# Recurrent memory attention with a gated feed-forward product on one Trainium2 core: banks of the memory products, and the turn of k's map

## The chip, the cores and the metric

The kernel runs on one core of one Trainium2 chip. The core has five engines that each work through a queue of their own in order: TensorE (matmul; PE in the profile, its weight loads PEld), VectorE (DVE), ScalarE (ACT), GpSimd (POOL) and SyncE (SP, which here only issues transfers). Matmuls write into PSUM, eight banks of 128 x 512 fp32. The metric is the device time of one execution in microseconds; the kernel before has a median of 699.38 us over three runs (699.01 to 701.35).

## The reference

The input x is 2048 x 512. It is normalised, and two branches are computed from it: attention with a memory that is carried over four segments of 512 rows (32 heads of 16), and a feed-forward branch of 1792 columns with a ReLU. The output is x plus the product of the two.

```python
xn = _layernorm(x, axis=-1)
for s in range(N):                      # N = 4 segments of L = 512 rows
    logits = einsum("bhqd,bhkd->bhqk", qs, ks) * scale + mask
    a_dot = softmax(logits) @ vs
    pq = phi(qs)                        # phi(t) = t + 1 for t > 0, else exp(t)
    num = einsum("bhld,bhde->bhle", pq, M)
    den = einsum("bhld,bhd->bhl", pq, z)[..., None] + 1e-6
    o = g * num / den + (1.0 - g) * a_dot
    pk = phi(ks)
    M = M + einsum("bhld,bhle->bhde", pk, vs)
    z = z + pk.sum over rows
s = concat(o) @ wo
g = silu(relu(xn @ w1) @ w2)
return x + s * g
```

## The kernel before, in words

Everything is in fp32. Large matrix products are split into a high and a low part of each operand, so one product is three matmuls: high x high, high x low, low x high (`triple`, `lanes`). Each of these 128-row matmuls is again cut into a lower half (rows 0 to 63, L744) and an upper half (rows 64 to 127, L752), which run beside each other. The upper halves trail the lower ones through a queue of up to 14 (`back`); where the program must end a product at once it empties this queue, and the uppers then run without partners.

The work is cut into 16 blocks n = 4 s + g (segment s, group g of eight heads), each of two half blocks u = 2 n + q. For a block:

- `proj` multiplies x by 128 columns of wq and of wk. `projout` takes the result off its bank: ScalarE writes the high plane into a buffer F (L974), VectorE the low plane into another F (L975). Both are sent to DRAM (`sdq`, `sdk`; L978 the high plane twice, L979 the low one). There are four F buffers in all (`NF_ = 4`). phi of q (segments 1 to 3) and of k (segments 0 to 2) is made beside it (L984, L985, L992).
- `stack` fetches the planes back as score operands `qs`, `ks` (L1113). `rowmax` computes the scores once for the row maxima (L1139 on TensorE, two single banks at a time; L1145 on VectorE), which are transposed (L1163), sent out and back into `qs` (L1165, L1166).
- `expo` computes the scores again, transposed, into the **pair** `pt` of two banks (L1191), ScalarE takes the exponentials over both banks at once (L1202, L1208) and GpSimd cuts the triangle (L1198). `pv` multiplies by v (L1239) and ScalarE scales the result into a buffer F (L1254), from where it is sent to `nn` (L1262) and `dq` (L1267).
- For blocks of segments 0 to 2, `memory` turns phi(k) with VectorE (L1073) into `pkT`, and `memory2` multiplies it by v (32 matmul rows of L1096) and adds the result to the memory `MC` of its group.
- For blocks of segments 1 to 3, `spread` lays the memory and its denominators out in `MZ`, and `numden` multiplies phi(q) with it: numerators and denominators, one matmul each (L1025, L1026). ScalarE takes the numerators off (L1033, into the tile of phi(q)), VectorE the denominators (L1035, into a buffer F). From there they are sent on to the division in `combine`.

Of the eight PSUM banks, six are single (`ps`), two form the pair `pt`. Before the change `numden` writes the two halves of the pair.

The order of all this is written out: the kernel records operations and plays them back in an order that a table (`ORDER`) fixes; two more tables fix the bank of each result (`BANKS`) and the yes-or-no answers of the recording code (`CHOICES`), and `PLAN` the sequence of weight loads. Each engine's queue follows that order, so a wait at the head of a queue holds up what stands behind it. SP issues nearly all transfers, and a waiting transfer holds up the later ones. The costs in `KINDS` and the due times are only used where the tables are made, not in the run.

Of the kernel before, what the change touches and what calls it, by code (L numbers as in the profile page):

```python
# [8 lines left out]
F32 = mybir.dt.float32  # L9
# [7 lines left out]
L = 512  # L17
# [29 lines left out]
WARM = 1  # L47
ONPAIR = True
# [29 lines left out]
ORDER = (
    "0AzAyAxwFABtAsUEqVppVTnUTZkCSXhSWSeSgAiRRdAcdTbTfTWYACaOTYASTDALTQPLLEALL+AIOILEHKHIAGKBAJFbDADYDJHICJERNjGJAgDA"
    "eBdDCbbgbFaHDYPVGHYFMEVVNNCSMYUKORCTQBPQJOOaRUYSTWMQkMQnPkLNLiJagLXaQJXaAVNcXTTQWXJJPPTPIPJP3OASNLVHNOLJrHLeKAJ)"  # L80
    "AGGLIJJKJxKIIJLJOMIIGLJJGIPJKQKOLKLJGLIIHGIVGGLSGGPLGNGOMJJOKJKLJFVLIQNRF2FRJMIJFKJHsIVIHuI!toJnKJHImuLtHJdvIFdb"
    "GL%abfbv?oagsttapFng!rrnFg/k1YbJtxYjG3qY+ht+YrgFajhlWYygrgVqYecnYYkbalgdXdWamcbcaaiFZgciFdHTUaTXFpZeWmdbwkWZTRgT"
    "qlf2AViSQbyRSuZtcpVc^HRDlPW^CTDixRTviRSDtfQqQSDbvRnXUYSqjVfDQTRKPbQPZDwRbLe*!DYPpXD/Tn/vOntGNkGwMii7EhLEf2DKOJJG"
    "mdhE-FGa8GZVEgFs>GRdDkdmcHP5kqQkDY1z(YfkqYOXcZoGqlDZMmkbYlUOcgUNSbZYZFRQRWVDXdEOVQfQULJDvKT6JNOr2NUoDMHTkGzQitAQ"
    "JtqROFZSaFjZrwSWrtQoVoFVlNOFzVsRWOTCJSMnLn!LJJNkgN-eUdoQRCRP3PIX=jX0INexNJbJQZLJOoMNmNlCkPSPCeKDE6NubL5sQ2tLCxrt"
    "LVrsMoykUWvpMjhmLqhDjwCofthmtnfehfmiJdJsDkhePUmQSYQjc1WiEHSTvEcFRKX6QXpCW1PDm2akOT+LRRwxCRCt+SYqHA6BWFtOBTCNRNwD"
    "RJNtCVECIBFkBP&hRBL@EMiBJOCKIQCBSCQBQPCRJBTQIBNUSKNK2QCOINyJMqPRIOCfojecOqNapRimECqBfnimBxmwh0puyloh7nh+p58F5uMb"
    "B5uH/CBu3-91wFzWBX6vuF4j3sxxpwDtoTBrmapqTDnnBl2shtLmWMVmBirBWihIngvfklSr3jo1j2j7SizkJhRtiAAzzjwpWtjsJ7Vlqplb32Ov"
    "jyuxoeR8AFxbj6vw2jPVyAxgIDAEgXXeCEabKeZZBLZPYJLKYECAH#OGVCMLDFoAEpAqnMG3Czm1y{k0p)]mxkFB&u(Kt:E$!rE9[i]{/([pzp]$"
    "+7B)@,tDA5v2AB4/&978k?$66z>@By3c>Bb2pgA52k2BU0zVqUybkApuoall7xcyaTqmdUepildtTlkrbjyeYmnug5lfpBX3i06i0lYWvkXW1lwW"  # L90
    "dv^Ldo^JtjsV5SqAkh2jhkfrhqCejrZephccQuXjlQcpjkocAcPS6BaTSAa1OYsWANTBSMMSQnSQAKANMTALdMcLWO1OAWuKxt]vAR]1clA$y#p!"
    "IAz5n03BxmAjkALE+rk1ood5Aidkw0kdylKJuJ2lml1cnzmaxAQjYtiqrXmkjPIihabffDZ^ojh^mgroOeinFXgkB^aZifWWAW^QnXVAMXM^bSgV"
# [76 lines left out]
def emit(tc, PE, ACT, DVE, POOL, SP, cst, ps, dr, args):  # L169
# [30 lines left out]
    def dve(cols, rd, wr, fn, dl, per=1.05e-3):  # L200
        return S.op("DVE", 0.14 + cols * per, rd, wr, fn, dl)
# [1400 lines left out]
```

## Time and profile before

| what | value |
| --- | --- |
| median of the runs (lowest, highest) | 699.38 us (699.01, 701.35) |
| profiled execution: its own time, its span | 700.62 us, 698.9 us |
| TensorE, VectorE, ScalarE, GpSimd busy | 686.7, 497.6, 408.2, 448.5 us |
| mean granted TensorE clock | 0.996 |
| transfers | 141.46 MB in 126451 packets, mean 202 GB/s |

The span runs from the first to the last profiled instruction. A row of a timeline has its start in us, its length, engine, line, operation, output <- inputs and count, and in brackets the idle time ahead of it on its engine and what ended it. A row of the waits has the engine, its line and tile, what it waited for, and then total us, how often, and the longest. A row of the groups has a count, then busy time and mean ns of one, then the idle time before. A row of the chain of waits has its start, its length and what it is; a transfer there runs from its issue to its landing.

### The profile page before, as it was taken

How to read it: one execution, taken by the hardware profiler on the slowest of the kernel's cores; microseconds unless marked ns; L12 is line 12 of the kernel's file. 1: busy time of each engine (PE TensorE's matmuls, PEld its weight loads, DVE VectorE, ACT ScalarE, POOL GpSimd, SP SyncE). 2: the span in 40 equal slices, each digit the busy share in tenths (PEclk: the TensorE clock that was granted, in tenths of full speed). 3: DMA queues.
4: the chain of work that ended last, by engine and by line, in shares of the span. 5: the costliest groups of instructions: out<-in, count | busy, mean ns of one | idle time of the engine just before them, and what ended most of it. 6: DMA issues, size and time to landing. Idle time of an engine off the chain costs nothing.

```text
span 698.9 us, 18573 instructions
## 1 busy us (share of the span) xinstructions
PE 686.7 (98%) x6770; PEld 558.8 (80%) x6770; DVE 497.6 (71%) x1592; ACT 408.2 (58%) x621; POOL 448.5 (64%) x570
## 2 busy tenths in 40 slices
PE   9999999999999999999999999899999999999996
PEld 8898888777787797878788778698778978777775
DVE  4188988797879876587777878575857557656247
ACT  5545665655777664576566584655665555675721
POOL 4553674554656776684687957567575776666674
PEclk9999999999999999999999999999999999999999
DMA  5795567466668667765775577775567797754433
GB/s 167 224 298 177 190 202 231 138 183 216 204 224 250 205 201 248 250 211 177 226 244 151 178 236 237 256 207 173 164 188 217 222 306 233 231 179 135 113 82 121
DMA packets 126451, 141.46 MB, mean 202 GB/s; under 512 B 24904, under 2 KB 70216, under 8 KB 126360
## 3 DMA queue, kind: packets, MB, share of 16 engines
q1 hardware_dynamic: 126152, 140.07, 65.1%
q8 instruction: 54, 0.88, 0.5%
q14 instruction: 37, 0.30, 0.1%
q10 hardware_dynamic: 208, 0.20, 0.1%
HBM read 99.01 MB, written 34.93 MB: 192 GB/s over the span
## 4 chain that ended last, share of the span: by engine, by line
PE 79%; DMA 10%; DVE 3%; POOL 2%; issue 2%; ACT 2%; SPq 1%; DVEq 0%; POOLq 0%; ACTq 0%
PE ps L744 45%; PE ps L752 10%; PE ps L1239 8%; PE ps L1139 6%; PE pt L1191 5%; DMA sdq<-F 2%; DMA ks<-sdk 2%; PE pt L475 1%; DMA nn<-F 1%; DMA io<-in_B_w_dram 1%; DMA dd<-F 1%; PE pt L1025 1%; DMA out_dram<-io 1%; DVE none L1145 1%; DMA sdk<-F 1%
## 5 line engine op out<-in xcount | busy, mean ns | idle before, releaser
L1145 DVE CUSTOM_DVE_ANT_0 none<-ps,causal 128x512 bf16<-128x512 f32 (+3 forms) x512 | 249.5, 487 | 67.4 <-PE ps L1139 45.3
L411 POOL TENSOR_TENSOR wl<-io,wh 128x512 fp32r<-128x512 f32 x176 | 227.9, 1304 | 106.9 <-ACT wh L410 90.1
L1208 ACT ACTIVATE P<-pt 128x1024 f32<-128x1024 f32 x128 | 131.2, 1025 | 78.0 <-PE pt L1191 47.9
L752 PE MATMUL ps<-xl,wh 64*128 64x512 f32 x352 | 141.6, 402 | 0.0
L744 PE MATMUL ps<-xh,wh 64*128 64x512 f32 x352 | 141.3, 402 | 0.0
L752 PE MATMUL ps<-xh,wl 64*128 64x512 f32 x352 | 137.3, 390 | 0.0
L752 PE MATMUL ps<-xh,wh 64*128 64x512 f32 x352 | 136.9, 389 | 0.0
L744 PE MATMUL ps<-xh,wl 64*128 64x512 f32 x352 | 136.6, 388 | 0.0
L744 PE MATMUL ps<-xl,wh 64*128 64x512 f32 x352 | 136.5, 388 | 0.0
L410 ACT ACTIVATE wh<-io 128x512 fp32r<-128x512 f32 x176 | 106.1, 626 | 44.0 <-PE ps L752 27.1
L1198 POOL TENSOR_SCALAR_AFFINE_SELECT P<-P 128x512 f32<-128x512 f32 x128 | 80.9, 650 | 41.4 <-ACT P L1208 28.8
L744 PE MATMUL ps<-wh,hh 64*128 64x512 f32 x224 | 91.0, 406 | 0.0
L752 PE MATMUL ps<-wl,hh 64*128 64x512 f32 x224 | 90.4, 404 | 0.0
L744 PE MATMUL ps<-wl,hh 64*128 64x512 f32 x224 | 87.5, 390 | 0.0
L744 PE MATMUL ps<-wh,hl 64*128 64x512 f32 x224 | 87.2, 389 | 0.0
L752 PE MATMUL ps<-wh,hl 64*128 64x512 f32 x224 | 87.1, 389 | 0.0
L752 PE MATMUL ps<-wh,hh 64*128 64x512 f32 x224 | 87.0, 388 | 0.0
L1139 PE MATMUL ps<-ks,qs 64*128 64x512 f32 (+3 forms) x512 | 75.2, 336 | 1.6 <-DMA ks<-sdk 1.6
L1239 PE MATMUL ps<-P,vt 128*17 128x512 f32 (+3 forms) x1024 | 75.2, 434 | 0.0
L744 PEld LDWEIGHTS ps<-xh,wl 64*128 64x128 f32 x352 | 64.8, 184 | 7.4 <-issue 0.2
L1191 PE MATMUL pt<-qs,ks 64*128 64x384 f32 (+3 forms) x512 | 67.9, 310 | 2.9 <-DVE F L1035 2.7
L744 PEld LDWEIGHTS ps<-xh,wh 64*128 64x128 f32 x352 | 64.9, 184 | 6.9 <-issue 2.2
(179 smaller groups left out, 1764.4 us busy)
## 6 DMA issues: line engine op xcount, KB each, us to landing
io<-in_B_w_dram SPq DMA_DIRECT2D x112, 256.0 KB
qs<-sdq SPq DMA_DIRECT2D x32, 512.0 KB
ks<-sdk SPq DMA_DIRECT2D x32, 512.0 KB
sdq<-F SPq DMA_DIRECT2D x16, 512.0 KB
sdk<-F SPq DMA_DIRECT2D x16, 512.0 KB
io<-in_A_x_dram SPq DMA_DIRECT2D x28, 256.0 KB
io<-in_A_wv_dram SPq DMA_DIRECT2D x16, 256.0 KB
io<-in_A_wq_dram SPq DMA_DIRECT2D x16, 256.0 KB
```

The source lines that it names most:

```text
L410: act(512, [rk], [hk], lambda: ACT.activation(h, raw, AF.Copy), 7.0 + nsplit if early else 6.0)
L411: pool(512, [rk, hk], [lk], lambda: POOL.tensor_tensor(l, raw, r32(h), op=OP.subtract), 8.5 + 1.3 * nsplit if early else 25.4)
L475: PE.matmul(pw[:, :128], ident, ident, start=True, stop=True)
L744: i = PE.matmul(m[0], m[2][0][LO], m[2][1][LO], start=m[4], stop=False)
L752: PE.matmul(h[0], h[2][0][HI], h[2][1][HI], start=False, stop=h[5] is not None)
L1025: PE.matmul(pn, MZ[:64], f[:64], start=True, stop=True)
L1139: PE.matmul(two[a][0][:, o:o + w], qs[r, p, w - 128:w], ks[r, p, :w], start=True, stop=True)
L1145: dve(w + 40 + TTR, [pk, "causal"], [f"{dk}.{p}{a}{j}"], lambda p=p, j=j, o=o, w=w, a=a, pS=pS: DVE.tensor_tensor_reduce(none[:, :w], pS[: ...
L1191: PE.matmul(pT[:, a, o:o + w], ks[r, p, 128 * i:128 * i + 128], qs[r, p, 128 * i:], start=True, stop=True)
L1198: pool(512, ks, ks, lambda: POOL.affine_select(t, t, pattern=[[0, 4], [1, 128]], compare_op=OP.is_ge, fill=0.0, base=0, channel_multiplier ...
L1208: act(1024, tk, [both[p]], lambda: ACT.activation(P[:, 2 * p:2 * p + 2, :], pT, AF.Exp, scale=0.25), 18.5)
L1239: PE.matmul(pO[32 * b:32 * b + 17, 128 * i:], v, P[:, b, o:o + w], start=i == 0, stop=i == 3)
```

## The change

Three things change. First, `numden` takes two of the six single banks (`PDR.take(2)`) where it took the two halves of the pair, and the recording code asks for two more ready banks there (`ONPAIR = False`). Second, `memory` turns k's map by another way: one VectorE transpose of all 32 x 32 blocks in place of sixteen of 32 x 128, which leaves the blocks in the wrong partitions; the map then goes to DRAM in one transfer (`KDR`, two buffers) and comes back in four, each of which brings the blocks of 32 partitions to their place. `memory2` reads it under other indices; its matmuls are the same in size and number. Third, the four tables are new, and with them the order of the whole program.

```diff
-ONPAIR = True
+ONPAIR = False
...
+    KDR = Ring("kd", [128, L], F32, 2, dr)
...
-        (pn, nk), (pd, dk) = PDR.fixed(6), PDR.fixed(7)
+        (pn, nk), (pd, dk) = PDR.take(2)
...
-        tks = [f"{tk}.{a}{b}" for a in range(4) for b in range(4)]
-        pv = pk.rearrange("p (t a j) -> p a t j", a=4, j=32)
-        for i, k in enumerate(tks):
-            a, b = slice(32 * (i // 4), 32 * (i // 4) + 32), slice(32 * (i % 4), 32 * (i % 4) + 32)
-            dve(140, fk, [k], lambda a=a, b=b, i=i: DVE.transpose(pkT[a, :, b], pv[b, i // 4]), 4.0)
+        tks = [f"{tk}.{a}" for a in range(4)]
+        d, k = KDR.next()
+        dve(512, fk, tks, lambda: DVE.transpose(
+            pkT.rearrange("p a (t i) -> p a t i", i=32), pk.rearrange("p (t a j) -> p a t j", a=4, j=32)), 2.0)
+        dma(tks, [k], lambda: SP.dma_start(d, pkT.rearrange("p a n -> p (a n)")), 4.0, "put")
+        for a in range(4):
+            dma([k], [tks[a]], lambda a=a: SP.dma_start(
+                pkT[32 * a:32 * a + 32], d[:, 128 * a:128 * a + 128].rearrange("(b j) n -> j b n", b=4)), 4.0, "tr")
...
-                    PE.matmul(pm[r, :32], pkT[:, c, r], V[:, c, hd:hd + 2, 0:16],
+                    PE.matmul(pm[r, :32], pkT[:, b, 32 * c:32 * c + 32], V[:, c, hd:hd + 2, 0:16],
...
-    "fffbc60001aab2ab2abaaeaaba1041ebedd93ac75ddbdbecbf67c5ddc082777673bb1cef73bfef79f95fbcf8fbdeeabbe1dd8eee87f0fbbb"
+    "fffbc60001aab2ab2abaaeaaba1041ebedd93ac75dd9f77b3f6f3d7bbb9777767389dcef7773773fe7c9f7bdd77bdeef39c4ee76f7bc790f"
```

Line numbers shift: below the tables a line of the changed kernel up to `numden` is one lower (L974 is L973), from `memory2` on two higher (L1191 is L1193, L1254 is L1256). How the rows move is shown at three places.

ScalarE around the seventh taking-off of numerators (block 10, segment 2); `wh` are weights' high parts, `P` exponentials, `F` the buffers for planes and results. Before:

```order
L1208 ACTIVATE P_0_171<-pt 128x1024
L410 ACTIVATE wh_102<-io_124 128x512
L1208 ACTIVATE P_0_172<-pt 128x1024
L410 ACTIVATE wh_101<-io_123 128x512
L410 ACTIVATE wh_104<-io_125 128x512
L1254 ACTIVATE F_174<-ps_117,gsc 128x512
L1033 ACTIVATE pq_150<-pt,tiny,gcol 128x512
L410 ACTIVATE wh_103<-io_126 128x512
```

With the change:

```order
L1256 ACTIVATE F_176<-ps_116,gsc 128x512
L984 ACTIVATE pk_152<-pk_152 128x512
L409 ACTIVATE wh_101<-io_122 128x512
L1210 ACTIVATE P_0_173<-pt 128x1024
L409 ACTIVATE wh_104<-io_126 128x512
L1210 ACTIVATE P_0_174<-pt 128x1024
L409 ACTIVATE wh_102<-io_125 128x512
L1032 ACTIVATE pq_150<-ps_119,tiny,gcol 128x512
```

The scaled result of `pv` (L1254, now L1256) stood right ahead of the numerators and now stands seven rows ahead of them.

TensorE at the same place. Before:

```order
L1025 MATMUL pt<-pq_150,mz 128x512
L1026 MATMUL pt<-pq_150,mz 128x512
L744 MATMUL ps_115<-xh_128,wh_100 128x512
L752 MATMUL ps_116<-xl_130,wh_106 128x512
L744 MATMUL ps_115<-xl_130,wh_100 128x512
L752 MATMUL ps_116<-xh_128,wl_113 128x512
L744 MATMUL ps_115<-xh_128,wl_107 128x512
L752 MATMUL ps_116<-xh_128,wh_106 128x512
L1139 MATMUL ps_119<-ks_84,qs_81 128x256
L1139 MATMUL ps_118<-ks_84,qs_81 128x256
```

With the change:

```order
L1024 MATMUL ps_119<-pq_150,mz 128x512
L1025 MATMUL ps_118<-pq_150,mz 128x512
L743 MATMUL ps_116<-xh_128,wh_103 128x512
L751 MATMUL ps_115<-xl_130,wh_105 128x512
L743 MATMUL ps_116<-xl_130,wh_103 128x512
L751 MATMUL ps_115<-xh_128,wl_112 128x512
L743 MATMUL ps_116<-xh_128,wl_110 128x512
L751 MATMUL ps_115<-xh_128,wh_105 128x512
L1193 MATMUL pt<-qs_82,ks_85 128x384 x2
L1193 MATMUL pt<-qs_82,ks_85 128x128 x2
```

Before, twelve more half matmuls follow and then L1191, the next to write the pair. With the change the pair is written right there, and the next to write one of the two single banks is L743 on `ps_119`, after six more halves and four matmuls of L1141.

The first map on VectorE. Before:

```order
L992 SCALAR_TENSOR_TENSOR pk_152,zs_153<-ps_116,pk_152 128x512
L785 SCALAR_TENSOR_TENSOR hl_138<-ps_119,hh_132 128x512
L1073 STREAM_TRANSPOSE pkT_160<-pk_152 32x4x32 x10
L785 SCALAR_TENSOR_TENSOR hl_139<-ps_115,hh_133 128x512
L1073 STREAM_TRANSPOSE pkT_160<-pk_152 32x4x32
L785 SCALAR_TENSOR_TENSOR hl_140<-ps_118,hh_134 128x512
```

With the change:

```order
L991 SCALAR_TENSOR_TENSOR pk_152,zs_155<-ps_114,pk_152 128x512
L1070 STREAM_TRANSPOSE pkT_162<-pk_152 128x512
L784 SCALAR_TENSOR_TENSOR hl_138<-ps_119,hh_132 128x512
L784 SCALAR_TENSOR_TENSOR hl_141<-ps_115,hh_135 128x512
L784 SCALAR_TENSOR_TENSOR hl_139<-ps_117,hh_133 128x512
```

Sixteen rows became one. On SP's queue the changed program has five rows more for each map; around block 6's planes they stand so (`kd` is the map in DRAM, `io` a load of weights or gate):

```order
L1264 DMA nn_180<-F_177 16x512 x3
L1074 DMA pkT_162<-kd_154 32x4x128
L1264 DMA nn_180<-F_177 16x512
L978 DMA sdq_144<-F_179 128x512
L977 DMA sdk_146<-F_176 128x2x512
L1074 DMA pkT_162<-kd_154 32x4x128 x2
L978 DMA sdk_146<-F_177 128x512
L1115 DMA qs_81<-sdq_144 128x2x512
```

One part of the map stands between results of `pv`, two between the planes of k.

More of the change, by code (lines that the diff above doesn't have):

```diff
@@ new lines @@
+    "b9c8eebb87abeeceee2773bbcfbe7def97df3bbaee1beec77779dc1f7cfdef8efb9dfeceebfbde7b3bbbb1ceef3ef9f7bef7bc11dd57c776"
+    "77713b9ff73fe7defbde7ef29f7bdd777777ce09cee9dcbbbbe73fe5f75de52beeceeeec77773e7ee77dcefefffe6c07bb2bb11998860576"
+    "4bb29d9d97609b0036598d88d93fd86cf5db393b2a765d903b2ec93184d86c26d8cb30821b0f5ca552ed9711b188d80e72ed93332360d714"
+    "a5d886c236079be360d86d98d83609b0b63611b041b08d8f576c9ce5c5764b950413662cc6cf5764bb29db39762bb2982c188c218f5712e2"
+    "9c570abffe0")
@@ new lines @@
+BANKS = (
+    "0123456454034120513413124015210523051453067350672506712675426751436750673136750067256751212367426742367026745067"
+    "4211672467345674025672540256720132670236702067245674546714367315671506751672156713453670406724367452673436715216"
+    "7151670056754231672436710413041356735267026745267306755306700367132672131671346730504236732506732567015672416753"
+    "4304213675067425671305567436725042367136705067316751367125467255672426704046704367405516740067412673506710672450"
+    "6741567010674134671236754254012054301556754467426734067256723513672346703367545067216750510126712546725567216742"
+    "1673404254122675367355673054670316743203670367433670467504671551672067121670303673026703401167355673021674167552"
+    "6712246743167346703306743067235167012673104567243675136714004105267031673526723346730674541670306712567536723367"
+    "1442672126712167050567303670525670546705132674336720674025670146745167350167026735026753267467673670567267467167"
+    "6753301472316")
@@ L78 @@
 ORDER = (
[L79 to L88, printed above, removed]
@@ new lines @@
+    "SNOUSQRcQEeaPReaaRXZbUSXWVTRfASMdPPPSMLYVOVNwTTDuSSMUVPKOlfSgihhgDVecfQckdDLebcOchbaRfheIddYfXkbDMcaaaMebbMHLWbV"
+    "YLYUZbZYIZWVjVAVHYSTGHQZENEEWPejMVcKLKIYPJIDMaLQC?PCWOUVQcCSPPYCOXQVPOOHQQGCFIKEKNKJCQDNGIWGCHGVEGJFCgEVHQIUEETS"
+    "GJPTWOGURESHCUCMCEQNKLULLEKEcCdHaLkMCaYPKYCVHULCcGDQecQTCcPZYZHCgjEpghWMnVCQjCkhPWfgMVDUDRacjOCPPWeSYPMHTRPWKYI_"
+    "FNNJUCMXPSPLGPHNiP0UJfTSJcHJIZZCHXXHOLCEVCKRSKKPDDJObDMNYCCLKCFRKGFPLTEMNQIMNMFLMKIGSMJQJGGOHMJarHRADHFEEFMQEJEJ"
+    "cIBXwdBuCbFgCBX1XUCyRZdUUEend4CBbGjOEmgvYNmXjtBM0MUsqEYWcCrYVXXSmfWebKkbafjfRZeReccYbDwXsDYsUJWTNbmdKWBiLfBfFTwW"
@@ new lines @@
+    "hmbsgBRcGnbQQGKYHhdTeNGLVbHXUPWaWUYURSoVYOQkgZHYWGduUeUUUnNGcfViGKcfjdfgcAShfcdjhcSVYVdcAIaXI^SJXR^RIVZXV^MQWOIU"
+    "N^GTIReTSMZALPO{W^dLN^dN(AR%OMMKLKJAIBYHCYWGAHWUBERUARDUDDBNNW%o%TCRM?MhCdKPrftqNSqvNMomao3CnY0WczJOxrJ4ubpd3Aca"
+    "ylwoa?kmoaMb-jMwflBgZAjUHYTGkWNtGUaHwpPSGsmAQkPpPPOmJNejMMRvUFqauWUqYSoFVmjkFQUXNNSPAKgYZNKEVaIUcGWMVYGVXDGCWSJT"
+    "RSAPCTSOAAGRrRGEJCSEDBQPIFBFGKFPFAMFETEEENDGkLeiKPDgOcqHZJMFlaWL-LUaDJXJ@qDVAnUCVUaXPSZGWqbEVpNaETUXBaSTMRWBKDaV"
+    "SDLbSCRKXMQNUPVAFQbU:LJVMWJESPSEKLJOJJIURK^QQRWMJPJI@NKIPL^COGMMCJKDOJIEBDJAEhHC=GBCEjbBHmACAkdsCjBpA0gEAAwQcruv"
@@ L118 @@
+    "CULABFFIFHAGeJAdcFEcCZUAaXDaYIABXKSVAXAWZAYDRDjOUPgQNOiOhPJUAWNABTAJPFIAEAJEEAIACAEEBGDBDDFBAAAEEBACEABBBACABAAA")
 RSTEP = (((0, 3, 0),), ((0, 0, 0), (0, 2, 128)), ((0, 1, 0), (1, 1, 256)), ((1, 0, 0), (1, 2, 128)), ((1, 3, 0),))
```

69 lines of the change are left out of this document (26 added, 43 removed), and 2 rows, old and new, of the table KINDS.

## The prediction

> **What bounds the kernel now.** I read the page's busy times and its chain first, to see whether one engine sets the end; then the waits of TensorE alone, to see how little of its time is idle and who causes that; then the timeline around the longest of those waits.
>
> ```profile
> span 698.9 us, 18573 instructions
> PE 686.7 (98%) x6770; PEld 558.8 (80%) x6770; DVE 497.6 (71%) x1592; ACT 408.2 (58%) x621; POOL 448.5 (64%) x570
> PE 79%; DMA 10%; DVE 3%; POOL 2%; issue 2%; ACT 2%; SPq 1%; DVEq 0%; POOLq 0%; ACTq 0%
> ...
> PE pt L1191 <- DVE F L1035: 2.7, 2, 2.1
> PE ps L1139 <- DMA ks<-sdk: 1.6, 2, 0.8
> ```
>
> TensorE is busy for 686.7 of 698.9 us and carries 79% of the chain that ended last. Its list of waits is short: the largest entry (total us, times, longest) is the score matmul of L1191, which writes the pair of banks, held up by the VectorE eviction of the denominators at L1035, twice. The change removes no matmul, so what it can win is TensorE's waits and any slot that holds half a matmul pair; what it does to VectorE's 497.6 us counts only where TensorE waits for it.
>
> The longest wait, by the timeline:
>
> ```profile
> 444.66 0.39 PE L744 MATMUL ps<-xh,wh 64*128 64x512 f32 x1
> 444.89 0.39 PE L744 MATMUL ps<-xl,wh 64*128 64x512 f32 x1
> 445.11 0.39 PE L744 MATMUL ps<-xh,wl 64*128 64x512 f32 x1
> 445.35 0.69 ACT L1254 ACTIVATE F<-ps,gsc 128x512 f32<-128x512 f32 x1 [2.08 <-DMA sdq<-F]
> 445.93 0.77 ACT L1033 ACTIVATE pq<-pt,tiny,gcol 128x512 f32<-128x512 f32 x1
> 446.74 0.81 DVE L1035 TENSOR_SCALAR F<-pt,gcol,tiny 128x512 f32<-128x512 f32 x1 [3.20 <-ACT pq L1033]
> 447.60 0.79 PE L1191 MATMUL pt<-qs,ks 64*128 64x384 f32 x4 [2.10 <-DVE F L1035]
> 448.84 0.63 PE L744 MATMUL ps<-wh,hh 64*128 64x512 f32 x1
> 449.27 0.63 PE L744 MATMUL ps<-wl,hh 64*128 64x512 f32 x1
> 449.69 0.62 PE L744 MATMUL ps<-wh,hl 64*128 64x512 f32 x1
> ```
>
> Read upwards from 447.60: the score matmuls wait for both banks of the pair; L1035 empties one and is the second of two evictions that take turns; L1033 empties the other but stands in ScalarE's queue behind L1254, and L1254 stood 2.08 us because its buffer F was still being sent out. That transfer is the first row here; the others are used below.
>
> ```profile
> 438.97 6.29 DMA sdq<-F
> ...
> 161.45 4.72 DMA sdk<-F
> 166.23 4.75 DMA ks<-sdk
> ...
> 185.27 2.13 DMA sdq<-F
> ```
>
> It landed at 445.26. Then the second cost of the wait: before it a matmul pair starts every 0.23 us, after it every 0.43. The stretches (length, TensorE, weight loads, VectorE, ScalarE, GpSimd, granted clock, DMA share, GB/s) show why:
>
> ```profile
> 420.00:440.00 20.00, 20.00 (x196) 16.49 (x192) 17.90 (x59) 9.48 (x16) 11.79 (x16) 1.00 0.81 246
> 440.00:460.00 20.00, 17.90 (x190) 13.81 (x188) 10.63 (x39) 11.96 (x18) 15.23 (x16) 0.91 0.67 216
> ```
>
> The granted clock fell to 0.91 on average, so 0.09 x 20 = 1.8 us of clock were lost. The other wait on L1035 is shorter and costs no clock:
>
> ```profile
> 276.60 0.69 ACT L1254 ACTIVATE F<-ps,gsc 128x512 f32<-128x512 f32 x1 [1.83 <-DMA sdq<-F]
> 277.86 0.39 PE L744 MATMUL ps<-wh,hl 64*128 64x512 f32 x1
> 278.85 0.50 PE L1191 MATMUL pt<-qs,ks 64*128 64x384 f32 x4 [0.59 <-DVE F L1035]
> ```
>
> **The change part by part.** *Pair to two single banks.* The first wait cost 447.60 - 445.11 - 0.23 = 2.26 us and 1.8 us of clock, about 4.0; the second 278.85 - 277.86 - 0.23 = 0.76. Together 4.8 us, the most this part can give. It gives nothing if the wait goes to whoever needs the single banks next: in the new order that is a score-maximum matmul (L1141) or a chain, after about as little TensorE work as before (at the place shown in the order, twelve half matmuls and two groups of score matmuls now, eighteen halves and one group then). And a new wait of this sort elsewhere would cost 4.0 again, so the bounds are a gain of 4.8 and a loss of 4.0. What decides is ScalarE's queue, since the cause was a buffer F in flight. In the old order L1254 stands right ahead of the eviction; in the new one its counterpart L1256 stands seven rows ahead. Counting TensorE's rows at the trace's paces, I estimate that the F buffer of this L1254 was refilled 5 us of TensorE work after it was filled; in the new order no L1256 follows a plane's transfer by under 10 us. The long case should not come back. The short one had an estimated 15 us, and two L1256 near these matmuls now have 14, so I leave its 0.76 us in. I take a gain of 4.0.
>
> The Trainium skill ("TensorE: Matmul & The Clock Gate", section Why this matters for your kernels) says that gaps of TensorE up to about 3 us leave the clock alone. By it the 2.10 us wait would have cost 2.26 us and no clock, and the gain would be 2.3 instead of 4.0. The trace disagrees: the clock fell after a wait of 2.10 us, so the row is used.
>
> *Half pairs.* The old order runs the queue of upper halves (L752) dry once in mid-program: six uppers without partner, then six lowers. The new order does this only at the start and the end, as the old one also does.
>
> ```profile
> 555.72 0.39 PE L752 MATMUL ps<-wh,xh 64*128 64x512 f32 x1
> 555.94 0.39 PE L752 MATMUL ps<-wl,xh 64*128 64x512 f32 x1
> 556.62 0.39 PE L752 MATMUL ps<-wl,xh 64*128 64x512 f32 x1
> 556.75 0.40 PE L744 MATMUL ps<-wh,oh 64*128 64x512 f32 x1
> ```
>
> From 555.94 the uppers are alone until the first lower starts at 556.75: 0.81 us. Six slots of 0.23 = 1.4 us would be the upper bound, nothing the lower. I take 0.8.
>
> *One transpose for sixteen.*
>
> ```profile
> L1073 DVE STREAM_TRANSPOSE pkT<-pk 32x128 f32<-32x128 f32 x192 | 58.1, 303 | 4.5
> ...
> L1163 DVE STREAM_TRANSPOSE mT<-mm 128x32 f32<-128x32 f32 x32 | 6.6, 207 | 10.8 <-POOL mm L1154 10.6
> ```
>
> Row length sets the time: 128 columns take 303 ns and 32 take 207, so 1.0 ns a column; 512 columns come to 303 + 384 = 687 ns. Twelve make 8.2 us where 192 x 303 ns = 58.1 stood: VectorE loses 49.9 us, which lie beside TensorE's work. Of TensorE's waits above only L1035's name VectorE, and those come from ScalarE. I take nothing; bounds 0 and a gain of 1.4 us (half the 2.7).
>
> *Sixty more transfers on SP's queue.* Twelve maps go out whole (256 KB) and come back in four parts of 64 KB. The legs are dependent. The nearest rows are the planes' transfers above, twice as large, at 2.13 to 6.29 us a leg; two legs, the transpose and five issues make some 6 to 16 us. From k's last projection matmul to the map's first use the new order has at least 28 us of TensorE work (an estimate from its rows at the trace's paces; 25 in the old order), so the work of chains and scores covers the route; if that cover goes, the whole rest shows, at the memory matmul. What stands behind the transfers in SP's queue matters more.
>
> ```profile
> SPq L399 <- POOL wl L411: 50.9, 36, 6.7
> ...
> SPq L979 <- DVE F L975: 9.3, 8, 2.3
> ...
> 451.66 0.37 SPq L1113 DMA_DIRECT2D ks<-sdk  x1
> 444.17 0.59 SPq L1166 DMA_DIRECT2D qs<-mx  x1
> ```
>
> An issue takes 0.37 to 0.59 us, so sixty are 22 to 35 us, and SP has that room: it stands 50.9 us on one reason alone. A transfer to DRAM waits for its VectorE result at the head of the queue for 1.2 us on average (9.3 over 8). Late are then weight loads, score planes and maxima. Only three of the sixty stand between a k plane's transfer and its stack load, where the two legs of 4.72 and 4.75 us leave little: 3 x 0.59 = 1.8 us at worst (thirteen stand behind q's planes, which are ready earlier). Traffic rises by 12 x 0.5 MB = 6 MB. I take nothing; bounds 0 and a loss of 1.8.
>
> *The rest of the new order.* The stack loads' wait (1.6 us) is taken as unchanged.
>
> Sum: 4.0 + 0.8 = 4.8 us less. Of the span that is 698.9 - 4.8 = 694.1; the profiled execution took 700.62 in all, so 695.8. The median of the runs before is 699.38, 1.24 under the profiled one, and I forecast for the median: **694.6 us**.
>
> **The rivals.** *More comes off.* Both evictions' waits (4.8), the half pairs at their bound (1.4) and the waits on stack loads (1.6) go: 7.8 us, 691.6. For it: VectorE's 49.9 us also shorten what ScalarE and SP wait for. Against it: L1139's waits end at a transfer, and transfers increase. Chance 0.17.
>
> *The wait only moves.* The next user of a single bank waits as the scores did, or ScalarE stands at L1256 and holds the exponentials: the 4.0 comes back, the half pairs' 0.8 stays: 698.6. For it: the same two evictions still follow the same matmuls as closely. Against it: the greater distance of F's refills. Chance 0.20.
>
> *VectorE stands at F; slower.* F has four buffers. The new order has VectorE write k's lower plane (L974) into the buffer of q's upper plane, in two places, an estimated 3.3 us of TensorE work after q's was done; the closest such case in the old order has 5.9. q's plane must first be sent out, 2.13 to 6.29 us after an issue. With the median of those rows (4.7) and an eviction and an issue of 0.5 us each VectorE would stand some 2 us, with the maxima of L1147 behind it, whose banks TensorE needs. It decides where VectorE stands longer than the 2 us or so of work before such a bank's next use; then a wait costs what the one at 447.60 did, 4.0. Two of these, one at a denominator that reuses F after 1.3 us, and 1.8 on SP make 13.8: 694.6 + 13.8 = 708.4; with two of the three, 704.4. Against it: the old order has a denominator's F reused after 0.9 us, without a wait on TensorE. Chance 0.19.
>
> **How the numbers follow.** Forecast 0.44, more 0.17, moved 0.20, slower 0.19. Of the forecast's cases 0.02 end within 0.3% of before, which is about what a measurement of this kernel can tell from no change (2.1 us: 697.3 to 701.5). So faster 0.42 + 0.17 = 0.59, the same 0.22, slower 0.19. The forecast's own range is 692 to 697: the half pairs' bounds, and the short wait gone or doubled. The range for 8 in 10 reaches down past the first rival by its unknown VectorE gain and up into the slower case as far as one 4.0 wait over before: 689 to 703.
>
> **What would show it.** Right: no TensorE wait on L1034 or L1032 over 1 us, granted clock 1.00 between 420 and 480 us, twelve transposes of about 0.69 us, no wait of the memory matmul (L1098) on a transfer. Wrong: a TensorE wait of about 2 us on any engine with a clock under 1.00 beside it, or VectorE idle before L974 with a plane's transfer as the cause. The forecast is wrong if TensorE's busy time does not fall under 685 us (686.7 less the 1.8 of clock).

## The result, and the profile after

The changed kernel took 695.37 us (median of 6 runs, 692.75 to 699.18) beside 699.64 us for the kernel before on the same chip: a ratio of 0.9950, 95% interval 0.9927 to 0.9972. Two later timings of the same two kernels gave 0.9956 (0.9938 to 0.9974) and 0.9941 (0.9920 to 0.9963). So it is faster by 0.4 to 0.6%, 3.1 to 4.1 us in the three timings; the forecast was 694.6. One of the eight executions of the second timing took 834.03 us at a mean granted clock of 0.754 and is left out of its ratio.

The profiled execution of the changed kernel is the slowest of its six (699.18, span 697.5). First two lines of its page, then the waits of TensorE (total us, times, longest; three dots stand for rows left out):

```profile
span 697.5 us, 18533 instructions
PE 684.1 (98%) x6770; PEld 563.7 (81%) x6770; DVE 449.2 (64%) x1412; ACT 407.8 (58%) x621; POOL 448.5 (64%) x570
```

```profile
PE ps L1141 <- DMA ks<-sdk: 1.9, 3, 0.7
PE ps L1141 <- issue: 1.8, 3, 0.8
PE ps L1141 <- DMA qs<-sdq: 1.6, 1, 1.6
...
PE ps L743 <- DVE md L1147: 1.1, 1, 1.1
PE ps L1141 <- DMA io<-in_B_w_dram: 0.7, 1, 0.7
PE ps L1098 <- DMA pkT<-kd: 0.3, 1, 0.3
```

The wait of the exponentials' scores on the denominators' eviction, 2.7 us before, is not in this list, and nothing has taken its place at the evictions of the single banks (L1032, L1034). VectorE is 48.4 us less busy. What has grown is L1141, the matmuls that need the stack loads: 6.0 us where the profile of before had 1.6 (3.5 of the 6.0 name a stack load, 1.8 name nothing that the profile shows). The memory matmul L1098 waited once for a returned map, 0.3 us. The clock around the place of the old wait, and the transposes (length, TensorE, weight loads, VectorE, ScalarE, GpSimd, granted clock, DMA share, GB/s; then busy us and mean ns of one):

```profile
440.00:460.00 20.00, 20.00 (x233) 16.35 (x226) 13.90 (x46) 12.77 (x19) 14.27 (x16) 1.00 0.84 256
```

```profile
L1070 DVE STREAM_TRANSPOSE pkT<-pk 128x512 f32<-128x512 f32 x12 | 8.5, 706 | 0.0
```

The missing wait of the pair, the clock and the transposes are as forecast. The growth at L1141 and the wait of L1098, short as it is, are not. Whether the missing wait is the reason for the gain is another matter: one profile of each kernel can't say whether the old wait was there in other executions too.

### The profile page after: what moved, and what is told of

Read it like the earlier page. It is cut to its first block, busy times and chain, and to the rows that moved or that the text cites. A ratio compares the mean times of both kernels' runs of the same rounds, so it can differ in the third digit from the quotient of the medians.

```text
span 697.5 us, 18533 instructions
## 1 busy us (share of the span) xinstructions
PE 684.1 (98%) x6770; PEld 563.7 (81%) x6770; DVE 449.2 (64%) x1412; ACT 407.8 (58%) x621; POOL 448.5 (64%) x570
## 4 chain that ended last, share of the span: by engine, by line
PE 82%; DMA 9%; DVE 3%; SPq 2%; issue 2%; POOL 1%; ACT 1%; DVEq 0%; POOLq 0%; ACTq 0%
PE ps L743 41%; PE ps L751 16%; PE ps L1241 8%; PE ps L1141 5%; PE pt L1193 4%; DMA ks<-sdk 3%; DVE none L1147 2%; PE ps L1024 1%; PE pt L474 1%; DMA dd<-rq 1%; PE ps L699 1%; SPq L1264 1%; DMA kd<-pkT 1%; PE ps L700 1%; DMA io<-in_B_w_dram 1%
## 5 line engine op out<-in xcount | busy, mean ns | idle before, releaser
L1147 DVE CUSTOM_DVE_ANT_0 none<-ps,causal 128x128 bf16<-128x128 f32 (+3 forms) x512 | 249.8, 488 | 85.2 <-PE ps L1141 60.5
L743 PE MATMUL ps<-xh,wh 64*128 64x512 f32 x352 | 141.7, 403 | 1.1 <-DVE md L1147 1.1
L743 PE MATMUL ps<-xl,wh 64*128 64x512 f32 x352 | 136.7, 388 | 0.0
L743 PE MATMUL ps<-xh,wl 64*128 64x512 f32 x352 | 136.5, 388 | 0.0
L743 PE MATMUL ps<-wh,hh 64*128 64x512 f32 x224 | 89.9, 401 | 0.0
L743 PE MATMUL ps<-wl,hh 64*128 64x512 f32 x224 | 86.9, 388 | 0.0
L743 PE MATMUL ps<-wh,hl 64*128 64x512 f32 x224 | 86.9, 388 | 0.0
L1141 PE MATMUL ps<-ks,qs 64*128 64x384 f32 (+3 forms) x512 | 73.3, 331 | 6.0 <-DMA ks<-sdk 1.9
L784 DVE SCALAR_TENSOR_TENSOR hl<-ps,hh 128x512 fp32r<-128x512 f32 x56 | 38.2, 686 | 54.8 <-ACT hh L783 54.4
L743 PEld LDWEIGHTS ps<-xh,wh 64*128 64x128 f32 x352 | 65.0, 185 | 8.8 <-issue 2.6
L743 PEld LDWEIGHTS ps<-xh,wl 64*128 64x128 f32 x352 | 64.8, 184 | 7.2
```

Source lines behind the costliest of these rows:

```text
L743: i = PE.matmul(m[0], m[2][0][LO], m[2][1][LO], start=m[4], stop=False)
L784: dve(512, [pk, hk], [lk], lambda: DVE.scalar_tensor_tensor(hl, ph, 0.0, r32(hh), op0=OP.max, op1=OP.subtract), 10.6)
L1141: PE.matmul(two[a][0][:, o:o + w], qs[r, p, w - 128:w], ks[r, p, :w], start=True, stop=True)
L1147: dve(w + 40 + TTR, [pk, "causal"], [f"{dk}.{p}{a}{j}"], lambda p=p, j=j, o=o, w=w, a=a, pS=pS: DVE.tensor_tensor_reduce(none[:, :w], pS[: ...
```

## The experiments

Most of the edits change the order in which the same operations are issued: the list of operations that the table of numbers has put in order goes through a small function before it is issued. Their kernels have a few more lines, so line numbers are shifted; the operation's tiles tell which is which. Operations that such a function has to find carry a tag (`S.tag`), and not all lines that set a tag are shown. Of timelines only the rows that bear on the reading are shown. Gains in us are 699 times (1 - ratio), with the ratio's interval.

**Was the wait a property of the kernel? The transfer moved.** In the kernel before, one transfer alone is issued elsewhere: the send of q's upper plane of block 11, for whose buffer F the ScalarE instruction L1254 had stood 2.08 us.

```diff
+def rearranged(seq):
+    late = next(x for x in seq if x[1] == ("hi", 11, "q"))
+    out = []
+    for x in seq:
+        if x is not late:
+            out.append(x)
+        if x[1] == ("plane", 11, "q"):
+            out.append(late)
+    return out
```

> The kernel before, with one transfer moved and nothing else: the send of q's upper plane of block 11 (L978, sdq<-F), which the profile of before has issued at 438.97 us and landed at 445.26, and on which ScalarE's L1254 stood for 2.08 us, is issued right behind the ScalarE instruction that writes that plane. Theory A (the recorded one: the buffer F in flight caused the wait of the pair and the loss of clock): no wait of L1191 on L1035 of about 2 us near 447, granted clock 1.00 in 440 to 460, some 3.5 to 4 us less, 695.5 to 696 where before has 699.4. Rival B (VectorE's 58.1 us of transposes are what delays the eviction L1035): the wait stays, 699.4. Rival C (the time goes to the next wait in the chain, so a single wait is worth nothing): the wait is gone and the time within 1 us of before.

Measured: ratio 0.9997 (0.9976 to 1.0017), a gain of 0.2 us, between -1.2 and 1.7. By the time this is rival C. The place itself did change. ScalarE's counterpart of L1254 is L1273 here, the evictions are L1052 and L1054:

```profile
444.79 0.68 ACT L1273 ACTIVATE F<-ps,gsc 128x512 f32<-128x512 f32 x1
445.37 0.78 ACT L1052 ACTIVATE pq<-pt,tiny,gcol 128x512 f32<-128x512 f32 x1
446.18 0.81 DVE L1054 TENSOR_SCALAR F<-pt,gcol,tiny 128x512 f32<-128x512 f32 x1 [0.54 <-ACT pq L1052]
```

```profile
440.00:460.00 20.00, 20.00 (x233) 15.34 (x226) 14.19 (x50) 14.53 (x21) 16.76 (x17) 1.00 0.81 262
```

L1273 stands no more, L1052 follows at once, the clock is whole. Set beside the profile of before, matmul by matmul, this execution was 2.0 us behind at 418 us and 1.8 us ahead at 451: 3.8 us came off in this place, as forecast. But it had lost 2.0 us ahead of it, in other waits, and its span is 698.2 against 698.9. So either the time goes elsewhere whenever a wait is taken away, or the profile of before had an execution with an uncommonly long wait; the comparison of two single executions can't tell.

**Two more profiles of the kernel before** decide between these.

> The kernel before, unchanged, for a second profiled execution. Theory A (the wait of the pair near 447 us, 2.26 us and 1.8 us of clock, is the kernel's own): L1191 waits there for L1035 again by 1.5 us or more, with pairs of matmuls every 0.43 us behind it. Theory D (formed after the moved transfer gave no time: the wait depends on how long one transfer takes in one execution, and other executions lose as much elsewhere): in at least one of this profile and the next the wait is under 1 us and the clock whole, with a span still within 1% of 698.9.

> The kernel before, unchanged, for a third profiled execution. Theories and numbers as for the second: A has the wait near 447 us at 1.5 us or more in each profile, D has it under 1 us in at least one of them, at a span of 692 to 706.

The same place in the second and the third profile (spans 695.1 and 697.4 us):

```profile
442.25 0.69 ACT L1254 ACTIVATE F<-ps,gsc 128x512 f32<-128x512 f32 x1 [0.24 <-DVE md L1145]
442.84 0.77 ACT L1033 ACTIVATE pq<-pt,tiny,gcol 128x512 f32<-128x512 f32 x1
443.65 0.81 DVE L1035 TENSOR_SCALAR F<-pt,gcol,tiny 128x512 f32<-128x512 f32 x1 [0.87 <-ACT pq L1033]
444.57 0.45 PE L1191 MATMUL pt<-qs,ks 64*128 64x384 f32 x4
```

```profile
443.54 0.69 ACT L1254 ACTIVATE F<-ps,gsc 128x512 f32<-128x512 f32 x1 [1.03 <-DMA sdq<-F]
444.12 0.77 ACT L1033 ACTIVATE pq<-pt,tiny,gcol 128x512 f32<-128x512 f32 x1
444.93 0.81 DVE L1035 TENSOR_SCALAR F<-pt,gcol,tiny 128x512 f32<-128x512 f32 x1 [1.67 <-ACT pq L1033]
445.79 0.50 PE L1191 MATMUL pt<-qs,ks 64*128 64x384 f32 x4 [0.55 <-DVE F L1035]
```

The order of the chain is the same each time: L1254, L1033, L1035, L1191. Its length is not: ScalarE stood 2.08, 0 and 1.03 us for the transfer (in the second profile L1254 did not wait for it), TensorE 2.10, under 0.25 and 0.55 us. This is theory D. Only the first was long enough to cost clock. Over the kernel, TensorE's waits on L1035 were 2.7, 0.3 and 1.5 us in the three profiles. The place is the kernel's own, the size is that of one execution, and the mean over three profiles, clock included, is (2.7 + 1.8 + 0.3 + 1.5) / 3 = 2.1 us, half of what the forecast took.

The record has more than three executions for the clock, since each timed one is listed with its mean granted clock. A loss of 1.8 us in a span of 699 us leaves at most 0.9974. In the timings beside the experiments the kernel before has 0.999 or 1.000 in 34 of 51 executions, so at least two in three had no such loss; the changed kernel has this in all 20 executions that its three ratios use. On average 0.8 us of clock were lost before (0.9 with the transfer moved) and 0.2 with the change, the end of the program included, so the clock makes some 0.6 us of the gain.

**VectorE's time in the old order.** The kernel before with a single transpose, fifteen left out and no transfers.

```diff
-        for i, k in enumerate(tks):
...
-            dve(140, fk, [k], lambda a=a, b=b, i=i: DVE.transpose(pkT[a, :, b], pv[b, i // 4]), 4.0)
+        turn = lambda: DVE.transpose(
+            pkT.rearrange("p a (t i) -> p a t i", i=32), pk.rearrange("p (t a j) -> p a t j", a=4, j=32))
+        for i, key in enumerate(tks):
+            S.tag = ("none" if i else "turn", n)
+            dve(140, fk, [key], turn, 4.0)
```

> The kernel before, its order and its pair kept, with a single transpose of 512 columns where the first of the sixteen stood and the other fifteen left out, and no transfer added (so the 32x32 squares are not put in their places, and the sum over earlier blocks is another). It gives VectorE the 49.9 us without the transfers, in the old order; the new order without the transfers took 693.9. Theory A (VectorE's time is off the path): 698.5 to 700. Rival B (VectorE's time is the gain): 693 to 695.5. Between them, 695.5 to 698.5, both have a share: the order and the single banks have what lies between this time and 693.9.

Measured: 696.76 us, ratio 0.9966 (0.9951 to 0.9980): a gain of 2.4 us, between 1.4 and 3.4. It lies between the two theories, so both have a share. VectorE's 50 us were not free: about 5% of them shows. Its one profile has 0.6 us of waits on L1035's counterpart, against 2.7, 0.3 and 1.5. All idle time of TensorE between its first and last matmul is not less (5.0 us against 5.8, 3.8 and 4.5), but its busy time is: 684.7 us where the profiles of before have 686.7, 685.0 and 686.6. As a matmul of 0.39 us starts every 0.23 us, a delay of up to 0.16 us stays hidden in the busy time, so many delays too short for the list of waits may have gone; that they did is not shown one by one.

**VectorE's time in the new order.** The changed kernel with sixteen transposes again, one behind each VectorE instruction that follows the first, and without the transfers.

```diff
+        sixteen = [lambda a=a, b=b: DVE.transpose(
+            pkT[32 * a:32 * a + 32, :, 32 * b:32 * b + 32], pv[32 * b:32 * b + 32, a])
+            for a in range(4) for b in range(4)]
...
+        if tag and tag[0] == "turn":
+            owed = [("DVE", None, f) for f in EXTRA[tag[1]]]
+        elif eng == "DVE" and owed:
+            out.append(owed.pop(0))
```

> The changed kernel with its order and its single banks, but the map made the old way: sixteen transposes of 32x128, the first where the one stood and one more behind each following VectorE instruction; the five transfers per map are left out. Theory A (the gain is the order's and the banks', the map is neutral): the changed kernel's time, 695.4 with 1.5 us to either side. Rival B (VectorE's 49.9 us are the gain): 698 to 700. Rival C (the transfers cost and hide part of the gain): 691.5 to 693.5, with the waits of TensorE on stack loads (L1141), 6 us in the changed kernel's profile, back at about 2.

Measured: 729.19 us, ratio 1.0428 (1.0401 to 1.0454), 30 us slower than the kernel before. TensorE now waits for the maxima again and again:

```profile
PE ps L1170 <- DVE md L1176: 14.4, 25, 1.3
PE ps L768 <- DVE md L1176: 3.3, 5, 1.2
```

None of the theories had this. The sixteen stand where this run puts them, so 33 us over the changed kernel is the price of these places and not the least that is possible; but it shows that the new order has no free 50 us of VectorE beside the maxima.

**The new map in the old order**, with its transfers: one transpose where the first of sixteen stood, the send next on SP, the returns behind the fifth to eighth SP instruction after it.

```diff
+        if tag and tag[0] == "turn":
+            put, *owed = EXTRA[tag[1]]
+            out.append(("SP", None, put))
+            seen = 0
+        elif eng == "SP" and owed:
+            seen += 1
+            if seen > 4:
+                out.append(("SP", None, owed.pop(0)))
```

> The kernel before, its order and its pair of banks kept; only the map is made the new way: one transpose of 128x512 where the first of sixteen stood, the send to DRAM as the next instruction on SP, the four returns behind the fifth to eighth SP instruction after it. Theory A: the map is neutral, 699.4 with 1.5 us to either side (VectorE about 50 us less busy, about 6 MB more moved). Rival B (the whole gain of the change is VectorE's time): 695 to 696. Rival C (the sixty transfers cost, by delaying stack loads and weights on SP's queue): 701 to 704, with TensorE waits on ks<-sdk or on wl grown by 2 us or more.

Measured: 720.78 us, ratio 1.0311 (1.0282 to 1.0340), outside the range of every theory. The waits of TensorE, and the longest of them (L1101 is the transpose, L1131 the memory matmul):

```profile
PE ps L1131 <- DMA pkT<-kd: 10.9, 3, 5.2
PE pt L1227 <- DVE F L1065: 4.6, 3, 1.9
```

```profile
507.50 0.71 DVE L1101 STREAM_TRANSPOSE pkT<-pk 128x512 f32<-128x512 f32 x1
508.24 0.33 SPq L1103 DMA_DIRECT2D kd<-pkT  x1
510.26 1.75 SPq L1104 DMA_DIRECT2D pkT<-kd  x4
513.86 0.66 PE L1131 MATMUL ps<-vt,pkT 128*32 128x32 f32 x32 [5.17 <-DMA pkT<-kd]
```

From the end of the transpose to the memory matmul it takes 513.86 - 508.21 = 5.65 us here, of which TensorE waits 5.17: the old order leaves 0.5 us for a route that takes 5.6, and at another map 2.0 us of 6.5. Long waits of this sort also cost clock (0.986 on average over the span, 0.996 in the profile of before). In the first profile of the changed kernel the shortest distance from a transpose's end to its memory matmul is 22 us. What the new order did was to make room for the route.

**The transfers left out, in the new order.** The changed kernel without its sixty transfers, and the changed kernel timed again.

```diff
+def rearranged(seq):
+    return [x for x in seq if not (x[1] and x[1][0] == "none")]
...
+        S.tag = ("none", n)
         dma(tks, [k], lambda: SP.dma_start(d, pkT.rearrange("p a n -> p (a n)")), 4.0, "put")
         for a in range(4):
+            S.tag = ("none", n)
             dma([k], [tks[a]], lambda a=a: SP.dma_start(
```

> The changed kernel with its single transpose of 512 columns, but without the five transfers that follow each (the sum over earlier blocks is then made from a map whose 32x32 squares are not put in their places, so that part of the result is another). Every other instruction is as in the changed kernel. Theory A (the transfers are neutral): 694.4 to 695.4, since at most the 0.3 us that the memory matmul waited once come off. Rival C (the transfers delay the stack loads on SP's queue and by their traffic): 691.5 to 693.5, with the waits of L1141 on stack loads at about 2 us where the changed kernel's profile has 6.

> The changed kernel, unchanged, timed beside the kernel before on the same chip as the next one, and profiled a second time (its first profiled execution was the slowest of its six runs). The ratio 0.995 should come again within 0.3%: 694 to 697. Theory D: waits of TensorE on stack loads (L1141) fall elsewhere than in the first profile and sum to 1 to 6 us; no wait of over 1.7 us, granted clock whole.

Without transfers: 693.93 us, ratio 0.9915 (0.9891 to 0.9940), a gain over before of 5.9 us (4.2 to 7.6). The changed kernel's second timing: 0.9956, 3.1 us, with waits on stack loads of 3.1 us (and 1.0 that name nothing) where the profile without transfers has 2.1:

```profile
PE ps L1141 <- DMA ks<-sdk: 3.1, 6, 0.9
...
PE ps L1141 <- issue: 1.0, 2, 0.7
```

```profile
PE ps L1153 <- DMA ks<-sdk: 2.1, 2, 1.5
```

693.93 lies between the ranges of the two theories, and the ratio's interval overlaps that of the changed kernel. Taken together the timings put the transfers' cost at about 2 us. How would it arise: by their place in SP's queue, or by their traffic?

**Queue or traffic.** The transfers a quarter as large, in the same places; the returns on ScalarE's queue; each transfer issued twice; and the changed kernel beside them.

```diff
-        dma(tks, [k], lambda: SP.dma_start(d, pkT.rearrange("p a n -> p (a n)")), 4.0, "put")
+        dma(tks, [k], lambda: SP.dma_start(d[:32], pkT[:32].rearrange("p a n -> p (a n)")), 4.0, "put")
...
-                pkT[32 * a:32 * a + 32], d[:, 128 * a:128 * a + 128].rearrange("(b j) n -> j b n", b=4)), 4.0, "tr")
+                pkT[32 * a:32 * a + 32, 0], d[:32, 128 * a:128 * a + 128]), 4.0, "tr")
```

```diff
-            dma([k], [tks[a]], lambda a=a: SP.dma_start(
-                pkT[32 * a:32 * a + 32], d[:, 128 * a:128 * a + 128].rearrange("(b j) n -> j b n", b=4)), 4.0, "tr")
+            dma([k], [tks[a]], lambda a=a: ACT.dma_start(
+                pkT[32 * a:32 * a + 32], d[:, 128 * a:128 * a + 128].rearrange("(b j) n -> j b n", b=4)), 4.0, "tr", "ACT")
```

```diff
+        out.append(x)
+        if x[1] and x[1][0] == "map":
+            out.append(x)
```

> The changed kernel, unchanged, as the measure for the three next ones on the same chip: 695 to 696.5.

> The changed kernel with its sixty transfers for the maps kept in number and in place, but each a quarter as large (the send takes 32 of 128 rows, each return 32 rows of 128 columns; the rest of the map isn't filled from there, so the sum over earlier blocks is another). Without any of them the time was 693.9. Theory Q (what they cost is their place and issue in SP's queue, ahead of stack loads): as the changed kernel, within 1 us. Theory T (what they cost is their traffic, beside which the other transfers take longer): 693 to 694.5.

> The changed kernel with the four returns of each map issued by ScalarE at the same place of the order, instead of by SP; the send stays on SP. Theory Q (SP's queue is what they cost): 693 to 695, unless ScalarE, which then stands at the first return until the send has landed, holds up the exponentials; in that case TensorE waits for P (L1210) or for ps by ScalarE, and the time is 697 or more. Theory T (traffic): no gain, 695 or more.

> The changed kernel with each of the sixty transfers for the maps issued twice in a row, 120 in all. If they cost some 2 us in the changed kernel (its 695.4 to 696.2 against 693.9 without them), twice as many should cost 2 to 3 us more: 697.5 to 699. If they cost nothing: within 1 us of the changed kernel.

The changed kernel 694.01 us (0.9941, 0.9920 to 0.9963); a quarter of the bytes 692.07 (0.9916, 0.9888 to 0.9944), as without any transfers; the returns on ScalarE's queue 694.32 (0.9940, 0.9919 to 0.9960), no gain. Both kernels were faster on this chip than the expectations supposed (the changed one 694.01 where 695 to 696.5 was expected), so the theories are judged by the distance to 694.01: as a bare number 694.32 would have fallen in theory Q's range. What moved, in the profile of the changed kernel and in that with quarters:

```profile
DMA packets 135091, 147.75 MB, mean 213 GB/s; under 512 B 25864, under 2 KB 77320, under 8 KB 135000
```

```profile
DMA packets 129331, 143.03 MB, mean 207 GB/s; under 512 B 25864, under 2 KB 72712, under 8 KB 129240
```

The issues on SP's queue are the same in the second, 4.7 MB are gone, and with them 1.9 us. SP's own standing for the landing of a send changes by less, from 1.6 to 0.8 us. So the timings speak for theory T: most of what the transfers cost goes with their bytes. The run with the returns on ScalarE's queue is weaker evidence than it looks, because the move made a wait of its own:

```profile
204.10 0.31 ACTq L1074 DMA_DIRECT2D pkT<-kd  x1
204.51 0.28 ACT L678 ACTIVATE vt<-ps 128x128 f32<-128x128 f32 x1 [4.05 <-DVE mv L512]
206.47 1.38 PE L1241 MATMUL ps<-P,vt 128*17 128x512 f32 x12 [1.02 <-ACT vt L678]
```

ScalarE has 4.05 us of idle time around the return, where the changed kernel's profile has 2.06 ahead of the same instruction; v comes late, and TensorE waits 1.02 us. A gain of about 1 us from the freed places on SP could be hidden behind it. By which of TensorE's waits the bytes cost time isn't shown either: the profiles have 1.0 us of waits on stack loads in the changed kernel on this chip and 1.3 with quarters. The size, some 2 us, is uncertain by about as much.

The doubled transfers took 823.1 us, 18% more than before, but this run measures something else than was meant:

```profile
SPq L1091 <- DMA pkT<-kd: 124.5, 48, 5.8
SPq L1088 <- DMA kd<-pkT: 42.6, 12, 5.7
```

The second copy of a transfer writes where the first does, so it stands at the head of SP's queue until the first has landed: 60 stops, 167 us. The expected 697.5 to 699 was missed by far. The run says nothing on twice the traffic, and much on what sixty stops of 2.8 us on average on SP cost: weight loads, planes and stack loads all stand behind it.

**The end of the program.** The profiles show one thing more that no experiment was needed for. The last instructions, before and after (the transfers that end the program follow them):

```profile
693.55 0.40 PE L702 MATMUL pt<-wh,ol 128*128 128x512 f32 x1
694.25 0.68 DVE L885 SCALAR_TENSOR_TENSOR io<-pt,io 128x512 f32<-128x512 f32 x1
694.96 0.69 DVE L887 TENSOR_TENSOR io<-io,bacc 128x512 f32<-128x512 f32 x1
```

```profile
693.49 0.28 PE L701 MATMUL pt<-wh,ol 128*128 128x256 f32 x1
693.80 0.42 DVE L916 SCALAR_TENSOR_TENSOR io<-pt,io 128x256 f32<-128x256 f32 x1
694.26 0.42 DVE L918 TENSOR_TENSOR io<-io,bacc 128x256 f32<-128x256 f32 x1
```

The new order has the half-wide pieces last. From the start of the last matmul to the end of the span it takes 697.46 - 693.49 = 3.97 us where before it took 698.87 - 693.55 = 5.32. It is 5.29 to 5.32 in all three profiles of before and 3.97 to 3.98 in all three of the changed kernel: 1.3 us, each time. No run moved these pieces alone.

## Why the prediction was right, and where it was not

The time was right: 694.6 forecast, 695.4, 696.2 and 694.0 measured, inside the forecast's own range of 692 to 697. Its sum was right in total only, and that is luck: two terms that were too small or missing on the gain's side and one on the loss's side made up for one that was twice too large. By the runs, the gain of 3.1 to 4.1 us is made of:

| part | forecast | by the runs |
| --- | --- | --- |
| VectorE's time (one transpose for sixteen) | 0 (0 to 1.4) | 2.4 (1.4 to 3.4), in the old order |
| order and single banks together | 4.8 | 5.9 - 2.4 = 3.5 (1.5 to 5.5) |
| sixty transfers | 0 (loss up to 1.8) | a loss of about 2 |

The split supposes that the parts add, across two timings on different chips and two orders. They need not: in the new order the same time of VectorE is worth far more than 2.4.

*Where the gain lies.* The prediction set out that the change "can win" TensorE's waits and slots that hold half a pair. The pages say otherwise:

| mean of three profiles, us | before | changed |
| --- | --- | --- |
| span | 697.1 | 694.7 |
| TensorE busy | 686.1 | 683.4 |
| last matmul's start to the end | 5.3 | 4.0 |
| idle time of TensorE between its first and last matmul | 4.7 | 6.2 |

TensorE waits 1.5 us more in the changed kernel, not less: the waits at L1141 took the place of the pair's. The gain is 2.7 us of busy time, with the same 6770 matmuls, and 1.3 us at the end. Of the 2.7, some 0.6 is clock and some 0.8 the half pairs. The rest would be delays too short to be listed as waits; this is argued from the sums and not shown row by row.

*Pair to two single banks.* The mechanism was right: transfer, L1254, evictions, L1191, seen again in the third profile, without the transfer and with hardly a wait in the second, and gone in all three of the changed kernel. The step that failed is the size, "I take a gain of 4.0": it is the wait of one execution, the others have 0.3 and 1.5 us in all, and at least two executions in three lose no such clock. The sum was made against the profiled execution, and the 1.24 us by which this one lay over the median was then taken off as if it belonged to something else, though the wait with its clock was more than all of it. Taking this transfer's wait away moved the median by 0.2 us (-1.2 to 1.7).

The change of banks itself couldn't be tried alone: in the old order, at eleven of the twelve places, none or one of the other six banks is free from the matmul to the evictions. So what the single banks give apart from the order stays open.

*Half pairs.* Forecast 0.8. The uppers run alone for 0.81, 0.80 and 0.80 us in the three profiles of before, and the new order has no such place in mid-program. The place is gone as forecast; what it was worth remains the estimate, as no run took it away alone.

*The end of the program* (1.3 us) had no term. The prediction read the order at the places where TensorE waits, and not its last rows, where every microsecond shows because nothing runs beside them. With the half pairs this makes 2.1 of the 3.5 us of the order and the banks. The remaining 1.4 is less than the uncertainty of the 3.5; what the pair's waits cost on average is of that size, but which part of it is theirs stays open.

*One transpose for sixteen.* Forecast 12 times 0.687 = 8.2 us; measured 0.706, 8.5 in all. That none of the 49.9 us would show is the second step that failed: its reason, that TensorE's list of waits names VectorE only through L1035, reads one execution's list of waits, and TensorE's busy time, which that list leaves out, is where the single transpose shows (684.7 us). And the new order leans on this time: with sixteen transposes back in it, in the places tried, it lost 33 us. As tried, neither half of the change was a gain of its own on the chip: the map alone cost 21 us, the order with sixteen transposes in the places tried 30, both together gained 3 to 4.

*Sixty transfers.* Forecast nothing, bound 1.8; about 2 us. "What stands behind the transfers in SP's queue matters more" isn't borne out: 48 of the 60 issues put on another queue gained nothing (with a new wait of 1.02 us that may hide some), and a quarter of the bytes in the same queue took the cost away. The bytes were counted (6 MB) and then not priced. The cover of 28 us for the route was right for the new order. "25 in the old order" was wrong for this purpose: it was counted from k's last projection, while at the tightest place the first of the old order's transposes leaves 0.5 us to the memory matmul.

*The stack loads* were taken unchanged at 1.6 us. The waits that name them were 1.6, 1.3 and 0.2 us in the profiles of before and 3.5, 3.1 and 1.0 in those of the changed kernel (all waits of the matmuls that need them: 1.6, 1.3 and 0.4 against 6.0, 4.1 and 3.1). So they grew, and the term was mis-sized. That the traffic alone did this isn't shown: without the transfers they are 2.1, with quarters 1.3.

*What would show it.* The signs named came true but for one: the memory matmul did wait for a transfer, once, 0.3 us. And two of them show less than was thought: the second profile of before has a busy TensorE of 685.0 us, at the bound, and it and the third have a clock of 1.00 in 440 to 460. A sign that the old kernel also gives in two of three executions separates nothing.

*The rivals.* "More comes off" (691.6) came true only where the transfers are left out or quartered, 692 to 694. "VectorE stands at F" did not happen, and "the wait only moves" not as it was meant: no wait of TensorE behind L1034, L1032 or L974 of over 0.3 us in three profiles. In small part the wait did move, to single banks that VectorE still read for the maxima (L1147): 1.1 and 0.5 us ahead of L743 in the first and second profile of the changed kernel, 1.4 ahead of L1141 in the third, against 0, 0 and 0.6 ahead of L637 in those of before.

## What to carry to other kernels

Before a wait is priced from a profile, look whether its length hangs on a transfer's duration; if so, the one profile gives its place and its mechanism, and its size needs more profiles, and the clocks of the timed executions beside them. Compare TensorE's busy time too and not only its waits: here the waits grew while the time fell. Read the last rows of the program in any change of order: there nothing runs beside the last piece. Two edits that each lose as tried can gain together, when one of them (the order) spends what the other (VectorE's time, room for a transfer's two legs) provides, so an order that was laid out for one way of computing is no ground for timing another.

## What the runs showed of the hardware that was not expected

**How long TensorE may stand before the clock falls.** The idles of TensorE in these profiles can be set beside the pace of the matmul pairs behind them. The single transpose in the old order (1.67 us, then a pair every 0.23 us), and the new map in the old order (1.88 us, then a pair every 0.42):

```profile
472.05 0.50 PE L1150 MATMUL ps<-ks,qs 64*128 64x512 f32 x2 [1.67 <-DMA nn<-F]
472.59 0.39 PE L754 MATMUL ps<-xh,wh 64*128 64x512 f32 x1
472.82 0.39 PE L754 MATMUL ps<-xl,wh 64*128 64x512 f32 x1
```

```profile
459.77 0.57 PE L1227 MATMUL pt<-qs,ks 64*128 64x384 f32 x4 [1.88 <-DVE F L1065]
460.78 0.62 PE L774 MATMUL ps<-wh,hh 64*128 64x512 f32 x1
461.20 0.62 PE L774 MATMUL ps<-wl,hh 64*128 64x512 f32 x1
```

Leaving the doubled transfers aside, no idle of 1.67 us or less was followed by the slow pace (1.62, 1.56 and 1.53 are the next), and all four of 1.88 us or more were (1.88, 2.10, 4.46 and 5.17). The granted clock was 0.50 over 3.4 us with the first two and over 6.8 us with the others, so the slow stretch does not end as soon as the matmuls run again. A wait that grows by 0.2 us across this step can cost 1.7 us more (half of 3.4). The doubled transfers, with their many waits, show that it isn't one sharp bound:

```profile
380.36 0.50 PE L1210 MATMUL pt<-qs,ks 64*128 64x512 f32 x2 [2.77 <-DMA qs<-mx]
380.70 0.39 PE L758 MATMUL ps<-xh,wh 64*128 64x512 f32 x1
380.94 0.39 PE L758 MATMUL ps<-xl,wh 64*128 64x512 f32 x1
```

Of the nineteen idles of 1.79 us or more in that profile that have pairs within 3 us behind them, only this one left the pace whole, and one of 1.46 us, 3 us behind another of 1.65, didn't. The Trainium skill ("TensorE: Matmul & The Clock Gate", section Why this matters for your kernels) puts the harmless gap at up to about 3 us. The row of 2.77 us agrees with it; the idles of 1.79 to 2.91 us that were followed by the slow pace, 1.88 and 2.10 among them, don't, and the prediction did well to go by the row; what else decides between them stays open.

**A few megabytes show.** 6.3 MB more in a program that moves 141 MB cost about 2 us (uncertain by about as much), although TensorE waited for none of it directly by more than 0.3 us in three profiles. Which waits it lengthens is not shown.
